# Hand-named PSUM banks and x transposed by DMA in a recurrent attention kernel

## The chip, the cores and the metric

The kernel runs on one core of a Trainium2 chip. The metric is the device time of one execution in microseconds (us); the kernel before takes 921.65 us (median of 3 runs, 919.34 to 922.05). Engines are called as in the profile: PE is TensorE (PEld its weight loads), DVE is VectorE, ACT is ScalarE, POOL is GpSimd, SP is SyncE, which here only issues DMAs.

## The reference, cut to what matters

```python
for s in range(n_seg):                          # 64 segments of 32 rows, strictly one after the other
    h = concatenate([mem, x[s*32:(s+1)*32]])    # 8 memory rows + 32 rows of x
    q, k, v = h @ Wq, h @ Wk, h @ Wv            # 32 heads of 128
    p = softmax(mask(q @ k.T * scale))
    o = (p @ v) @ Wo
    mem = o[:8]                                 # feeds the next segment
    outs.append(o[8:])
a = concatenate(outs)
b = gelu(layernorm(x) @ w1 + b1) @ w2 + b2      # independent of the recurrence
return g * a + (1 - g) * b                      # g = sigmoid(sum(x * gate_w))
```

The MLP `b` is computed first, in some 110 us. The 64 steps of the recurrence are the rest. Four steps make a *tile* of 128 rows of x.

## The kernel before

One step projects 32 rows (8 of memory, 24 of x) through Wq, Wk and Wv. The 8 rows of x left over in each of four steps are projected together for the next tile, as *side work*: units of four matmuls, 0.24 to 0.33 us each in the chain, put where PE would wait. The kernel divides PSUM, the memory that matmuls write, into eight banks. Seven rotate under one name; whoever asks takes the one used longest ago, and waits until it has been read out. The eighth holds the scores.

Some names from the code: hT is the step's transposed input, its memory rows first; QT, KT and V are its projections; E are the exponentials, R the reciprocals of their sums, Pm and Px the probabilities for memory rows and x rows; UTT is what enters the output projection and wsb what leaves it. GL are the left-over columns of a transposed tile of x, and QL, KL and VL their projections; VL takes the way through DRAM (vd).

```python
pb = loop.enter_context(tc.tile_pool(name="pb", bufs=7, space=PSUM))
ps = loop.enter_context(tc.tile_pool(name="ps", bufs=1, space=PSUM))
def bank(shape, dtype=FP32):
    return pb.tile(shape, dtype, tag="b", name="b")

def x_tr(T, x_sb):                       # x of a tile, transposed by PE
    xp = bank([P, KC, P], BF16)
    for kc in range(KC):
        nc.tensor.transpose(xp[:, kc, :], x_sb[:, kc * P:(kc + 1) * P], ident[:])
    def ev():                            # placed later in DVE's order
        ...                              # xT <- xp on DVE; GL <- left-over columns of xT on POOL
    dve_q.append(ev)
...
for s in range(nseg + 2):                # one step; the order of each engine is the order written
    ...
        prep_h(s + 1); prep_q(s); x_mul(s - 1)        # POOL: hT, QT columns, Px = E * R
    ...
            bk = bank([P, 512])                       # five Q/K banks, DVE transposes each out
    ...
            scores(S, s)                              # then two exponentials on ACT
            sm = bank([P, NG, 8])                     # sums, then run_fill(5): five side units
            run_fill(5)
            # DVE: reciprocal, Pm = E * R
            Um = [bank([P, NG, 8]) for _ in range(4)]
            av(Um, 8, s, V, Pm, 8, 0, 0)              # Pm.V for the memory rows
            sr = bank([P, NG, 32])                    # sums for the x rows
            # DVE: UTT <- Um, then the long reciprocal of sr
            run_fill(2)
    ...                                  # output projection, two halves, wsb <- wp by DVE and ACT
        if live and s >= 1:
            av_x(s - 1)                               # Px.V of the step before
        run_fill(1)
        if s + 1 < nseg:
            aT = bank([P, KC, M])                     # new memory, transposed
            ...
            nc.vector.tensor_copy(out=hn[:, :, 0:M], in_=aT[:])   # hT: the next step starts on it
            S_next = mask_mm()                        # mask into the score bank
        run_fill(1)
```

Of the kernel before, what the change touches and what calls it, by code (L numbers as in the profile page):

```python
# [23 lines left out]
def kernel(ctx, tc, A_x, A_mem0, A_Wq, A_Wk, A_Wv, A_Wo, A_seg_len, B_x, B_w1, B_b1, B_w2, B_b2, gate_w, out):  # L24
# [33 lines left out]
    x0_sb = pers.tile([P, Dm], BF16)  # L58

    with tc.tile_pool(name="mlpw", bufs=1) as mlpw, \  # L60
# [41 lines left out]
        nc.sync.dma_start(x0_sb[:], x2[0:P, :])  # L102
# [149 lines left out]
    pb = loop.enter_context(tc.tile_pool(name="pb", bufs=7, space=PSUM))  # L252
    ps = loop.enter_context(tc.tile_pool(name="ps", bufs=1, space=PSUM))
# [3 lines left out]
    def bank(shape, dtype=FP32):  # L257
        return pb.tile(shape, dtype, tag="b", name="b")
# [36 lines left out]
    dve_q, act_q = [], []  # L295

    def flush(q, n=1):
        for _ in range(min(n, len(q))):
            q.pop(0)()

    def x_load(T):
        if T == 0:
            return x0_sb
        x_sb = cw.tile([P, Dm], BF16, tag="xc", bufs=1, name="xc")
        nc.sync.dma_start(x_sb[:], x2[T * P:(T + 1) * P, :])
        return x_sb

    def x_tr(T, x_sb):
        xp = bank([P, KC, P], BF16)
        for kc in range(KC):  # L310
            nc.tensor.transpose(xp[:, kc, :], x_sb[:, kc * P:(kc + 1) * P], ident[:])

        def ev():
            xT = cw.tile([P, KC, P], BF16, tag="xT", bufs=3, name="xT")
            nc.vector.tensor_copy(out=xT[:], in_=xp[:])
            xTs[T] = xT
            GL = cw.tile([P, KC, 32], BF16, tag="GL", name="GL")
            nc.gpsimd.tensor_copy(out=GL[:].rearrange("p k (i c) -> p k i c", c=LEFT),
                                  in_=xT[:].rearrange("p k (i c) -> p k i c", c=seg)[:, :, :, RIDE:seg])
            GLs[T] = GL  # L320
        dve_q.append(ev)
# [3 lines left out]
    def left_qk(T, t, hf):  # L325
        h0, h1 = HF[hf]
        bk = bank([P, 512])
        for kc in range(KC):
            qk_unit(bk, GLs[T], t, h0, h1, kc)
            if kc < KC - 1:  # L330
                yield
        def ev():
            Tv = qk_tr(bk, h0, h1)
            if t == 0:
                nc.gpsimd.tensor_copy(out=QL[T % 2][:, h0:h1, :], in_=Tv)
            else:
                for hh in range(h0 // 8, h1 // 8):
                    r0 = 8 * hh - h0
                    nc.gpsimd.tensor_copy(out=KL[T % 2][:, :, :, hh, :], in_=Tv[:, r0:r0 + 8, :].rearrange("p g (s c) -> p g s c", c=LEFT))
        dve_q.append(ev)  # L340
        yield

    def left_v(T, vb):
        bk = bank([P, 512])
        for kc in range(KC):
            v_unit(bk, GLs[T], vb, kc)
            if kc < KC - 1:
                yield

        def ev():  # L350
            vt = cw.tile([P, 4, Dh], BF16, tag="vt", name="vt")
            nc.scalar.copy(out=vt[:].rearrange("p i e -> p (i e)"), in_=bk[:])
            if vb == 0:
                vds[T] = dr.tile([P, 4, 2, Dh], BF16, tag="vd", name="vd")
            nc.sync.dma_start(vds[T][:, 2 * vb:2 * vb + 2], vt[:].rearrange("p (a g) e -> p a g e", g=2))
            if vb == 1:
                src = vds.pop(T)[:].rearrange("(j s c) h g e -> j h c s (g e)", j=4, s=SPT)
                for j in range(4):
                    for hh in range(4):
                        r0 = 32 * j + LEFT * hh  # L360
                        nc.sync.dma_start(VL[T % 2][r0:r0 + LEFT].rearrange("p s g e -> p s (g e)"), src[j, hh])
        act_q.append(ev)
        yield

    def wo_left(T):
        bk = bank([P, Dm])
        for u in range(8):
            wo_unit(bk, UTT[T % 2], 32, u)
            if u < 7:
                yield  # L370

        def ev():
            w = cw.tile([P, Dm], BF16, tag="wsbL", bufs=1, name="wsbL")
            nc.scalar.copy(out=w[:], in_=bk[:])
            wsbLs[T] = w
        act_q.append(ev)
        yield

    def out_units(T):
        ob = bank([P, Dm])  # L380
        for si in range(SPT):
            nc.tensor.matmul(ob[32 * si:32 * si + 32, :], lhsT=SelX[:], rhs=wsbs.pop(SPT * T + si + 2)[:], start=True, stop=False,
                             tile_position=(0, 32 * si))
        yield
        if T + 3 < NT:
            x_tr(T + 3, x_load(T + 3))
            yield
        if T not in wsbLs:
            flush(act_q, 9)
        for si in range(SPT):  # L390
            nc.tensor.matmul(ob[32 * si:32 * si + 32, :], lhsT=SelL[si][:], rhs=wsbLs[T][:], start=False, stop=True,
                             tile_position=(0, 32 * si))

        def ev():
            o_sb = cw.tile([P, Dm], BF16, tag="o", bufs=1, name="o")
            nc.vector.scalar_tensor_tensor(out=o_sb[:], in0=ob[:], scalar=g_all[:, T:T + 1], in1=c_all[:, T, :], op0=ALU.mult, op1=ALU.add)
            nc.sync.dma_start(out2[T * P:(T + 1) * P, :], o_sb[:])
        dve_q.append(ev)
        yield

    def filler(T):

        if T + 1 < NT:
            for vb in range(2):
                yield from left_v(T + 1, vb)
            for hf in range(2):
                for t in range(2):
                    yield from left_qk(T + 1, t, hf)

        if T >= 1:  # L410
            yield from wo_left(T - 1)
            yield from out_units(T - 1)
        elif NT > 2:
            x_tr(2, x_load(2))
            yield
# [9 lines left out]
    def mask_mm():  # L425
        S = ps.tile([P, NG, EW], FP32, tag="S", name="S")
        nc.tensor.matmul(S[:], lhsT=ident[:], rhs=MkA[:].unsqueeze(2).to_broadcast([P, 4, 2, EW]),  # L427
                         start=True, stop=True, skip_group_check=True)
        return S

# [31 lines left out]
    m0p = bank([P, KC, M], BF16)  # L462
# [3 lines left out]
    x_tr(0, x_load(0))  # L466
    flush(dve_q)
    x_tr(1, x_load(1))
    flush(dve_q)
# [14 lines left out]
    S_next = mask_mm()  # L484
    Es, Rs, Pxs, Vs, Uxs = {}, {}, {}, {}, {}
    fill = iter(())

    def run_fill(n):
        for _ in range(n):
            if T + 1 < NT or si >= 2:  # L490
                next(fill, None)
# [10 lines left out]
    def av_x(s):  # L502
        U = [bank([P, NG, 32]) for _ in range(4)]
        av(U, 32, s, Vs.pop(s), Pxs.pop(s), 0, 32, 24)
        Uxs[s] = U

# [6 lines left out]
    for s in range(nseg + 2):  # L513
# [3 lines left out]
        if si == 0 and live:  # L517
            fill = filler(T)
        if live:
            S = S_next  # L520
            if s >= 2:
                ux_out(s - 2)
            if s + 1 < nseg and (s + 1) // SPT in xTs:
                prep_h(s + 1)
# [5 lines left out]
            for bi, (t, h0, h1) in enumerate(BANKS):  # L530
                bk = bank([P, 512])
                for kc in range(KC):
                    qk_unit(bk, hc, t, h0, h1, kc)
                Tv = qk_tr(bk, h0, h1)
                dst = QT[:, h0:h1, 0:32] if t == 0 else KT[:, h0:h1, :]
                (nc.gpsimd.tensor_copy if bi == 2 else nc.scalar.copy)(out=dst, in_=Tv)  # L536
            V = cw.tile([P, NG, Dh], BF16, tag="V", name="V")
            Vs[s] = V
            vb0, vb1 = bank([P, 512]), bank([P, 512])
# [3 lines left out]
            flush(dve_q)  # L543
# [10 lines left out]
            sm = bank([P, NG, 8])  # L554
# [8 lines left out]
            Um = [bank([P, NG, 8]) for _ in range(4)]  # L563
            av(Um, 8, s, V, Pm, 8, 0, 0)
            sr = bank([P, NG, 32])
            nc.tensor.matmul(sr[:], lhsT=BO[:], rhs=E[:, :, 16:48], start=True, stop=False, skip_group_check=True)  # L566
# [4 lines left out]
            nc.vector.reciprocal(out=R[:, 8 * NG:].rearrange("p (i q) -> p i q", q=32), in_=sr[:])  # L571
            run_fill(2)
        else:
            if s == nseg:
                ux_out(s - 2)
                x_mul(s - 1)
                av_x(s - 1)
            else:
                ux_out(s - 2)
            flush(dve_q)  # L580
            Tp, sp = divmod(s - 2, SPT)
        wsb = cw.tile([P, Dm], BF16, tag="wsb", bufs=7, name="wsb")
        for half in range(2):
            d = slice(256 * half, 256 * half + 256)
            wp = bank([P, 256])
# [5 lines left out]
        if s >= 2:  # L591
            wsbs[s] = wsb
        if live and s >= 1:
            av_x(s - 1)
        run_fill(1)
        if s + 1 < nseg:
            aT = bank([P, KC, M])
            for m in range(KC):
                nc.tensor.matmul(aT[:, m, :], lhsT=wsb[:, m * P:(m + 1) * P], rhs=Sel[:, 0:M], start=(m == 0), stop=True, skip_group_check=True)  # L599
            nc.vector.tensor_copy(out=hn[:, :, 0:M], in_=aT[:])  # L600
            S_next = mask_mm()
# [4 lines left out]
    for _ in filler(NT):  # L606
        flush(dve_q, 9)
        flush(act_q, 9)
# [12 lines left out]
    cnt = bank([1, 1])  # L621
# [121 lines left out]
```

## Time and profile before

| | kernel before |
|---|---|
| time | 921.65 us |
| span of the profiled run, mean granted PE clock | 920.6 us, 0.980 |
| PE busy | 832.7 us (90%) |
| tiles 2 to 13, mean us from each step's first score matmul to the next: steps 0-1, 1-2, 2-3, 3-0 | 12.01, 12.02, 12.18, 11.62 |
| the tile | 47.82 us |

The score matmuls come once a step, and the next scores depend on everything in between, so the distance from score to score shows where in a tile time comes or goes. The lines of the profile are in the prediction. A q behind an engine's name is its sequencer, and "issue" is time for which the profile shows no wait. In its lists "A <- B: total, times, longest" says that engine and line A waited for B. In the chain, each line is a piece of work on the path that ended last.

### The profile page before, as it was taken

To read this page: it belongs to the slowest core of one execution; us is meant where nothing else is said; L and a number is where in the kernel's file an instruction comes from. 1 tells how busy PE (TensorE), PEld (TensorE's weight loads), DVE (VectorE), ACT (ScalarE), POOL (GpSimd) and SP (SyncE) were. 2 spreads that over 40 slices of the span, in tenths; PEclk is the share of its full clock that TensorE was granted. 3 is DMA by queue.
4 is the path that set the end of the run, shared out by engine and by line. 5 is a ranking of instruction groups with operands and counts; after the bars stand their busy time and mean duration, and the time that the engine had idled before them with its cause. 6 is when DMAs were issued, how large, how long until landed. Compare 5 with 4: busy or idle time off the path is not lost.

```text
span 920.6 us, 49285 instructions
## 1 busy us (share of the span) xinstructions
PE 832.7 (90%) x22481; PEld 519.9 (56%) x22481; DVE 502.2 (55%) x999; ACT 443.2 (48%) x1252; POOL 257.1 (28%) x599
## 2 busy tenths in 40 slices
PE   1899738899999999999999999999999999999996
PEld 1566414555556566565656555656555566655554
DVE  4722214655556565556565656565656565655553
ACT  2666404454545445554544454555455545444453
POOL 1000172333333322333332323232323232323221
PEclk9999959999999999999999999999999999999998
DMA  9970001100000000010101000000000000000000
GB/s 281 421 260 1 7 1 31 27 9 26 15 27 15 27 16 26 10 32 10 32 5 37 5 27 14 28 14 23 19 21 21 15 27 15 27 15 21 10 4 17
DMA packets 29829, 37.77 MB, mean 41 GB/s; under 512 B 3592, under 2 KB 27504, under 8 KB 28080
## 3 DMA queue, kind: packets, MB, share of 16 engines
q1 hardware_dynamic: 29440, 34.30, 10.9%
q8 instruction: 178, 2.92, 1.3%
q0 software_dynamic: 176, 0.27, 0.2%
q14 instruction: 35, 0.29, 0.1%
HBM read 28.26 MB, written 6.29 MB: 38 GB/s over the span
## 4 chain that ended last, share of the span: by engine, by line
PE 81%; ACT 7%; issue 3%; DVE 3%; DMA 2%; POOL 2%; SPq 1%; ACTq 0%; POOLq 0%; DVEq 0%
PE b L269 32%; PE b L291 16%; PE b L280 12%; PE b L451 4%; PE bp L172 3%; PE hp L178 3%; ACT E L552 3%; PE b L456 2%; PE S L436 2%; PE b L566 1%; ACT wsb L590 1%; PE b L599 1%; PE b L555 1%; ACT UTT L511 1%; PE S L427 1%
## 5 line engine op out<-in xcount | busy, mean ns | idle before, releaser
L275 DVE STREAM_TRANSPOSE Tt<-b 128x512 f32<-128x512 f32 (+1 forms) x384 | 225.8, 613 | 97.4 <-PE b L269 85.1
L269 PEld LDWEIGHTS <-hT 128*32 128x32 bf16 x5120 | 134.1, 97 | 93.1 <-DVE hT L600 6.3
L291 PE MATMUL b<-Wo_sb,UTT 128*32 128x256 bf16 (+1 forms) x4736 | 166.4, 289 | 1.1 <-ACT UTT L511 0.8
L291 PEld LDWEIGHTS <-UTT 128*32 128x32 bf16 x4736 | 125.3, 98 | 26.9 <-issue 3.1
L269 PE MATMUL b<-Wq_sb,hT 128*32 128x512 bf16 x2048 | 132.9, 379 | 1.3
L280 PE MATMUL b<-Wv_sb,hT 128*32 128x512 bf16 x2048 | 133.9, 380 | 0.0
L269 PE MATMUL b<-Wk_sb,hT 128*32 128x256 bf16 (+1 forms) x3072 | 133.3, 308 | 0.0
L497 POOL TENSOR_TENSOR Px<-E,R 128x256 bf16<-128x256 bf16 x64 | 43.1, 674 | 258.1 <-DVE R L571 254.4
L571 DVE RECIPROCAL R<-b 128x256 f32<-128x256 f32 x64 | 112.0, 1749 | 4.2 <-PE b L567 4.2
L536 ACT CAST KT<-Tt 128x256 bf16<-128x256 f32 (+1 forms) x192 | 87.0, 476 | 54.1 <-DVE Tt L275 54.1
L536 POOL CAST QT<-Tt 128x512 bf16<-128x512 f32 x64 | 39.2, 612 | 189.7 <-DVE Tt L275 189.7
L590 ACT CAST wsb<-b 128x256 bf16<-128x256 f32 x66 | 24.6, 372 | 134.3 <-PE b L291 134.3
L536 ACT CAST QT<-Tt 128x512 bf16<-128x512 f32 x64 | 39.6, 618 | 98.7 <-DVE Tt L275 98.7
L511 ACT CAST UTT<-b 128x256 bf16<-128x256 f32 x256 | 77.0, 387 | 12.8 <-PE b L456 10.0
L559 DVE RECIPROCAL R<-b 128x64 f32<-128x64 f32 x64 | 35.7, 557 | 85.1 <-PE b L556 85.1
L280 PEld LDWEIGHTS <-hT 128*32 128x32 bf16 x2048 | 50.7, 96 | 28.2
L451 PEld LDWEIGHTS <-V 32*128 32x128 bf16 x4096 | 36.2, 91 | 50.8 <-DVE Pm L561 29.0
L600 DVE CAST hT<-b 128x32 bf16<-128x32 f32 x63 | 12.0, 191 | 90.3 <-PE b L599 90.3
L570 ACT CAST UTT<-b 128x64 bf16<-128x64 f32 x128 | 20.9, 215 | 77.5 <-PE b L456 77.5
L178 PE MATMUL hp<-yT,w_sb 128*128 128x256 bf16 (+1 forms) x352 | 52.5, 276 | 5.3 <-ACT hTm L179 3.5
L499 POOL TENSOR_TENSOR racc<-racc,R 128x320 f32<-128x320 f32 x64 | 55.1, 862 | 0.0
L179 ACT ACTIVATE hTm<-hp,b_sb 128x256 bf16<-128x256 f32 (+1 forms) x88 | 40.5, 470 | 29.2 <-PE hp L178 29.0
(110 smaller groups left out, 1087.1 us busy)
## 6 DMA issues: line engine op xcount, KB each, us to landing
Wq_sb<-in_A_Wq_dram SPq DMA_DIRECT2D x4, 1024.0 KB
Wk_sb<-in_A_Wk_dram SPq DMA_DIRECT2D x4, 1024.0 KB
Wv_sb<-in_A_Wv_dram SPq DMA_DIRECT2D x4, 1024.0 KB
Wo_sb<-in_A_Wo_dram SPq DMA_DIRECT2D x4, 1024.0 KB
vd<-vt SPq DMA_DIRECT2D x32, 128.0 KB
VL<-vd SPq DMA_DIRECT2D x256, 16.0 KB
out_dram<-o SPq DMA_DIRECT2D x16, 128.0 KB
xc<-in_A_x_dram SPq DMA_DIRECT2D x15, 128.0 KB
```

The source lines that it names most:

```text
L178: nc.tensor.matmul(hp[:rows, :], lhsT=w1_sb[:, kc, fc * P:fc * P + rows], rhs=yT[:, kc, :], start=(kc == 0), stop=(kc == KC - 1))
L179: nc.scalar.activation(out=hTm[:rows, fc, :], in_=hp[:rows, :], func=ACTF.Gelu_apprx_tanh, bias=b1_sb[:rows, fc:fc + 1], scale=1.0)
L269: nc.tensor.matmul(bk[32 * j:32 * j + 32, 0:n], lhsT=G[:, kc, :], rhs=W5[t][:, kc, h0:h1, j, :], start=(kc == 0), stop=(kc == KC - 1), til ...
L275: nc.vector.transpose(out=Tt[:, 0:n], in_=bk[:, 0:n])
L280: nc.tensor.matmul(bk[32 * j:32 * j + 32, :], lhsT=G[:, kc, :], rhs=Wv5[:, kc, 4 * vb:4 * vb + 4, j, :], start=(kc == 0), stop=(kc == KC - ...
L291: nc.tensor.matmul(bk[32 * g:32 * g + 32, :], lhsT=ut[:, i, j, c0:c0 + 32], rhs=Wo_sb[:, 4 * i + j, d0:d1], start=(j == 0 and i < 4), stop ...
L451: nc.tensor.matmul(U[j][:, i, :], lhsT=V[q, i, :], rhs=Pt[q, i, c_main:c_main + n], start=(i == 0), stop=False, skip_group_check=True, til ...
L497: nc.gpsimd.tensor_tensor(out=Px[:, :, 0:32], in0=E[:, :, 16:48], in1=Rr, op=ALU.mult)
L499: nc.gpsimd.tensor_tensor(out=racc[:], in0=racc[:], in1=R[:], op=ALU.add)
L511: nc.scalar.copy(out=UTT[T % 2][:, :, j, c0 + M:c0 + 40], in_=U[:])
L536: (nc.gpsimd.tensor_copy if bi == 2 else nc.scalar.copy)(out=dst, in_=Tv)
L571: nc.vector.reciprocal(out=R[:, 8 * NG:].rearrange("p (i q) -> p i q", q=32), in_=sr[:])
```

## The change

Its intent: no wait for a PSUM bank in the step. Five banks go round in the step in a written order, two serve side work, and the eighth holds in turn mask and scores, the sums, and the new memory. PE loses the transposes of x. The core of the diff:

```diff
-    pb = loop.enter_context(tc.tile_pool(name="pb", bufs=7, space=PSUM))
-    ps = loop.enter_context(tc.tile_pool(name="ps", bufs=1, space=PSUM))
+    pb = loop.enter_context(tc.tile_pool(name="pb", bufs=1, space=PSUM))
+    def bank(k, shape, dtype=FP32):
+        return pb.tile(shape, dtype, tag=f"b{k}", name=f"b{k}")
+    def side(shape, dtype=FP32):
+        side_n[0] += 1
+        while side_n[0] - 2 in side_todo:      # read-out of the bank's tenant not yet placed:
+            flush(dve_q)                       # place it here
+            flush(act_q)
+        return bank(5 + side_n[0] % 2, shape, dtype)
...
     def x_load(T):
-        if T == 0:
-            return x0_sb
-        x_sb = cw.tile([P, Dm], BF16, tag="xc", bufs=1, name="xc")
-        nc.sync.dma_start(x_sb[:], x2[T * P:(T + 1) * P, :])
-        return x_sb
+        xT = cw.tile([P, KC, P], BF16, tag="xT", bufs=3, name="xT")
+        for kc in range(KC):
+            nc.sync.dma_start_transpose(xT[:, kc, :], x2[T * P:(T + 1) * P, kc * P:(kc + 1) * P])
+        xTs[T] = xT
+        GL = cw.tile([P, KC, 32], BF16, tag="GL", name="GL")
+        nc.gpsimd.tensor_copy(out=GL[:]..., in_=xT[:]...)
...
+        if si == 1 and T + 2 < NT:
+            x_load(T + 2)                      # stands ahead of prep_h, prep_q and x_mul
...
-            sr = bank([P, NG, 32])
+            sr = B[:, 0:NG * 32].rearrange("p (i q) -> p i q", q=32)      # B: the score bank
...
+        if s + 1 < nseg:
+            S_next = mask_mm()                 # now before Px.V
         if live and s >= 1:
-            av_x(s - 1)
+            av_x(s - 1, (ne, na, nc_, nb))
         run_fill(1)
         if s + 1 < nseg:
-            aT = bank([P, KC, M])
+            aT = S_next[0][:, NG * EW:NG * EW + KC * M].rearrange("p (k m) -> p k m", m=M)
             ...
-            S_next = mask_mm()
         run_fill(1)
```

Side work is also re-dealt: the output rows of a tile are now assembled two tiles later, not one.

More of the change, by code (lines that the diff above doesn't have):

```diff
@@ L57 @@
     g_all = pers.tile([P, NT], FP32)
-    x0_sb = pers.tile([P, Dm], BF16)
     with tc.tile_pool(name="mlpw", bufs=1) as mlpw, \
@@ L101 @@
             nc.sync.dma_start(Wo_sb[:, i:i + hsplit, :], A_Wo[i:i + hsplit].rearrange("h e d -> e h d"))
-        nc.sync.dma_start(x0_sb[:], x2[0:P, :])
         make_identity(nc, ident[:])
@@ L250, with flush, later @@
                                     fill=MASK_NEG, base=M, channel_multiplier=-1)
-    pb = loop.enter_context(tc.tile_pool(name="pb", bufs=7, space=PSUM))
-    ps = loop.enter_context(tc.tile_pool(name="ps", bufs=1, space=PSUM))
+    pb = loop.enter_context(tc.tile_pool(name="pb", bufs=1, space=PSUM))
     dr = loop.enter_context(tc.tile_pool(name="dr", bufs=2, space=bass.MemoryType.DRAM))
     cw = loop.enter_context(tc.tile_pool(name="cw", bufs=2))
-    def bank(shape, dtype=FP32):
-        return pb.tile(shape, dtype, tag="b", name="b")
+    def bank(k, shape, dtype=FP32):
+        return pb.tile(shape, dtype, tag=f"b{k}", name=f"b{k}")
+    side_n, side_todo = [0], set()
+    dve_q, act_q = [], []
+    def flush(q, n=1):
+        for _ in range(min(n, len(q))):
+            k, ev = q.pop(0)
+            ev()
+            side_todo.discard(k)
+    def later(q, ev, k):
+        side_todo.add(k)
+        q.append((k, ev))
+    def side(shape, dtype=FP32):
[4 more added lines that the diff above has]
+        return bank(5 + side_n[0] % 2, shape, dtype)
     Wq5 = Wq_sb[:].rearrange("p k (h j e) -> p k h j e", h=H, j=4)
@@ L294 @@
     vds, xTs, GLs, wsbs, wsbLs = {}, {}, {}, {}, {}
-    dve_q, act_q = [], []
-    def flush(q, n=1):
-        for _ in range(min(n, len(q))):
-            q.pop(0)()
     def x_load(T):
-        if T == 0:
-            return x0_sb
-        x_sb = cw.tile([P, Dm], BF16, tag="xc", bufs=1, name="xc")
-        nc.sync.dma_start(x_sb[:], x2[T * P:(T + 1) * P, :])
-        return x_sb
-    def x_tr(T, x_sb):
-        xp = bank([P, KC, P], BF16)
-        for kc in range(KC):
-            nc.tensor.transpose(xp[:, kc, :], x_sb[:, kc * P:(kc + 1) * P], ident[:])
-        def ev():
-            xT = cw.tile([P, KC, P], BF16, tag="xT", bufs=3, name="xT")
-            nc.vector.tensor_copy(out=xT[:], in_=xp[:])
-            xTs[T] = xT
-            GL = cw.tile([P, KC, 32], BF16, tag="GL", name="GL")
-            nc.gpsimd.tensor_copy(out=GL[:].rearrange("p k (i c) -> p k i c", c=LEFT),
-                                  in_=xT[:].rearrange("p k (i c) -> p k i c", c=seg)[:, :, :, RIDE:seg])
-            GLs[T] = GL
-        dve_q.append(ev)
+        xT = cw.tile([P, KC, P], BF16, tag="xT", bufs=3, name="xT")
+        for kc in range(KC):
+            nc.sync.dma_start_transpose(xT[:, kc, :], x2[T * P:(T + 1) * P, kc * P:(kc + 1) * P])
+        xTs[T] = xT
+        GL = cw.tile([P, KC, 32], BF16, tag="GL", name="GL")
+        nc.gpsimd.tensor_copy(out=GL[:].rearrange("p k (i c) -> p k i c", c=LEFT),
+                              in_=xT[:].rearrange("p k (i c) -> p k i c", c=seg)[:, :, :, RIDE:seg])
+        GLs[T] = GL
     HF = ((0, H // 2), (H // 2, H))
@@ L326, in left_qk @@
         h0, h1 = HF[hf]
-        bk = bank([P, 512])
+        bk = side([P, 512])
+        side_k = side_n[0]
         for kc in range(KC):
@@ L339, in ev @@
                     nc.gpsimd.tensor_copy(out=KL[T % 2][:, :, :, hh, :], in_=Tv[:, r0:r0 + 8, :].rearrange("p g (s c) -> p g s c", c=LEFT))
-        dve_q.append(ev)
+        later(dve_q, ev, side_k)
         yield
     def left_v(T, vb):
-        bk = bank([P, 512])
+        bk = side([P, 512])
+        side_k = side_n[0]
         for kc in range(KC):
@@ L361, in ev @@
                         nc.sync.dma_start(VL[T % 2][r0:r0 + LEFT].rearrange("p s g e -> p s (g e)"), src[j, hh])
-        act_q.append(ev)
+        later(act_q, ev, side_k)
         yield
     def wo_left(T):
-        bk = bank([P, Dm])
+        bk = side([P, Dm])
+        side_k = side_n[0]
         for u in range(8):
@@ L375, in ev @@
             wsbLs[T] = w
-        act_q.append(ev)
+        later(act_q, ev, side_k)
         yield
     def out_units(T):
-        ob = bank([P, Dm])
+        ob = side([P, Dm])
+        side_k = side_n[0]
         for si in range(SPT):
@@ L384, in out_units @@
         yield
-        if T + 3 < NT:
-            x_tr(T + 3, x_load(T + 3))
-            yield
-        if T not in wsbLs:
-            flush(act_q, 9)
         for si in range(SPT):
@@ L397, in ev @@
             nc.sync.dma_start(out2[T * P:(T + 1) * P, :], o_sb[:])
-        dve_q.append(ev)
+        later(dve_q, ev, side_k)
         yield
@@ L403, in filler @@
         if T + 1 < NT:
-            for vb in range(2):
-                yield from left_v(T + 1, vb)
-            for hf in range(2):
-                for t in range(2):
-                    yield from left_qk(T + 1, t, hf)
+            yield from left_v(T + 1, 0)
+            yield from left_v(T + 1, 1)
+            yield from left_qk(T + 1, 0, 0)
+            yield from left_qk(T + 1, 1, 0)
+            yield from left_qk(T + 1, 0, 1)
+            yield from left_qk(T + 1, 1, 1)
+        if T >= 2:
+            yield from out_units(T - 2)
         if T >= 1:
             yield from wo_left(T - 1)
-            yield from out_units(T - 1)
-        elif NT > 2:
-            x_tr(2, x_load(2))
-            yield
     def prep_h(s):
@@ L425, in mask_mm @@
     def mask_mm():
-        S = ps.tile([P, NG, EW], FP32, tag="S", name="S")
-        nc.tensor.matmul(S[:], lhsT=ident[:], rhs=MkA[:].unsqueeze(2).to_broadcast([P, 4, 2, EW]),
+        B = bank(7, [P, 512])
+        S = B[:, 0:NG * EW].rearrange("p (i e) -> p i e", e=EW)
+        nc.tensor.matmul(S, lhsT=ident[:], rhs=MkA[:].unsqueeze(2).to_broadcast([P, 4, 2, EW]),
                          start=True, stop=True, skip_group_check=True)
-        return S
+        return B, S
     def scores(S, s):
@@ L461 @@
     nc.sync.dma_start(m0[:], A_mem0[0])
-    m0p = bank([P, KC, M], BF16)
+    m0p = side([P, KC, M], BF16)
     for kc in range(KC):
@@ L465 @@
     nc.vector.tensor_copy(out=hT[0][:, :, 0:M], in_=m0p[:])
-    x_tr(0, x_load(0))
-    flush(dve_q)
-    x_tr(1, x_load(1))
-    flush(dve_q)
+    x_load(0)
+    x_load(1)
     prep_h(0)
@@ L484 @@
     S_next = mask_mm()
+    ring = (0, 1, 2, 3, 4)
     Es, Rs, Pxs, Vs, Uxs = {}, {}, {}, {}, {}
@@ L489, in run_fill @@
         for _ in range(n):
-            if T + 1 < NT or si >= 2:
+            if T + 1 < NT or si >= 1:
                 next(fill, None)
@@ L500, in x_mul, with av_x @@
         Pxs[s] = Px
-    def av_x(s):
-        U = [bank([P, NG, 32]) for _ in range(4)]
+    def av_x(s, banks):
+        U = [bank(k, [P, NG, 32]) for k in banks]
         av(U, 32, s, Vs.pop(s), Pxs.pop(s), 0, 32, 24)
@@ L518 @@
             fill = filler(T)
+        if si == 1 and T + 2 < NT:
+            x_load(T + 2)
         if live:
-            S = S_next
+            B, S = S_next
+            na, nb, nc_, nd, ne = ring
+            ring = (nd, ne, na, nc_, nb)
+            qk_banks = (na, nb, nc_, nd, ne)
             if s >= 2:
                 ux_out(s - 2)
-            if s + 1 < nseg and (s + 1) // SPT in xTs:
+                flush(act_q)
+            if s + 1 < nseg:
                 prep_h(s + 1)
@@ L530 @@
             for bi, (t, h0, h1) in enumerate(BANKS):
-                bk = bank([P, 512])
+                bk = bank(qk_banks[bi], [P, 512])
                 for kc in range(KC):
@@ L538 @@
             Vs[s] = V
-            vb0, vb1 = bank([P, 512]), bank([P, 512])
+            vb0, vb1 = bank(na, [P, 512]), bank(nb, [P, 512])
             for kc in range(KC):
@@ L542 @@
             nc.scalar.copy(out=v_out(V, 0), in_=vb0[:])
-            flush(dve_q)
+            flush(dve_q, 9)
             for kc in range(2):
@@ L553 @@
             nc.scalar.activation(out=E[:, :, 16:EW], in_=S[:, :, 16:EW], func=ACTF.Exp, scale=scale, accum_out=hist[:, s, 1:2])
-            sm = bank([P, NG, 8])
+            sm = bank(nc_, [P, NG, 8])
             nc.tensor.matmul(sm[:], lhsT=BO[:], rhs=E[:, :, 8:16], start=True, stop=False)
@@ L562 @@
                                     in1=R[:, 0:8 * NG].rearrange("p (i q) -> p i q", q=8).unsqueeze(2).to_broadcast([P, NG, 2, 8]), op=ALU.mult)
-            Um = [bank([P, NG, 8]) for _ in range(4)]
+            Um = [bank(k, [P, NG, 8]) for k in (nd, ne, na, nc_)]
             av(Um, 8, s, V, Pm, 8, 0, 0)
-            sr = bank([P, NG, 32])
-            nc.tensor.matmul(sr[:], lhsT=BO[:], rhs=E[:, :, 16:48], start=True, stop=False, skip_group_check=True)
+            sr = B[:, 0:NG * 32].rearrange("p (i q) -> p i q", q=32)
+            nc.tensor.matmul(sr, lhsT=BO[:], rhs=E[:, :, 16:48], start=True, stop=False, skip_group_check=True)
             nc.tensor.matmul(sr[:, :, 24:32], lhsT=BO[:], rhs=E[:, :, 48:56], start=False, stop=True, skip_group_check=True)
@@ L570 @@
                 (nc.scalar.copy if j % 2 else nc.vector.tensor_copy)(out=UTT[Tp % 2][:, :, j, 24 - 8 * sp:24 - 8 * sp + M], in_=Um[j][:])
-            nc.vector.reciprocal(out=R[:, 8 * NG:].rearrange("p (i q) -> p i q", q=32), in_=sr[:])
+            nc.vector.reciprocal(out=R[:, 8 * NG:].rearrange("p (i q) -> p i q", q=32), in_=sr)
             run_fill(2)
@@ L576 @@
                 x_mul(s - 1)
-                av_x(s - 1)
+                av_x(s - 1, (ne, na, nc_, 7))
             else:
@@ L581 @@
             Tp, sp = divmod(s - 2, SPT)
-        wsb = cw.tile([P, Dm], BF16, tag="wsb", bufs=7, name="wsb")
+        wsb = cw.tile([P, Dm], BF16, tag="wsb", bufs=10, name="wsb")
         for half in range(2):
             d = slice(256 * half, 256 * half + 256)
-            wp = bank([P, 256])
+            wp = bank((nb, nd)[half], [P, 256])
             for u in range(8):
@@ L592 @@
             wsbs[s] = wsb
+        if s + 1 < nseg:
+            S_next = mask_mm()
         if live and s >= 1:
-            av_x(s - 1)
+            av_x(s - 1, (ne, na, nc_, nb))
         run_fill(1)
         if s + 1 < nseg:
-            aT = bank([P, KC, M])
+            aT = S_next[0][:, NG * EW:NG * EW + KC * M].rearrange("p (k m) -> p k m", m=M)
             for m in range(KC):
-                nc.tensor.matmul(aT[:, m, :], lhsT=wsb[:, m * P:(m + 1) * P], rhs=Sel[:, 0:M], start=(m == 0), stop=True, skip_group_check=True)
-            nc.vector.tensor_copy(out=hn[:, :, 0:M], in_=aT[:])
-            S_next = mask_mm()
+                nc.tensor.matmul(aT[:, m, :], lhsT=wsb[:, m * P:(m + 1) * P], rhs=Sel[:, 0:M], start=False, stop=True, skip_group_check=True)
+            nc.vector.tensor_copy(out=hn[:, :, 0:M], in_=aT)
         run_fill(1)
@@ L605 @@
                 pass
-    for _ in filler(NT):
+    flush(act_q, 9)
+    for _ in out_units(NT - 2):
         flush(dve_q, 9)
-        flush(act_q, 9)
+    for _ in wo_left(NT - 1):
+        pass
+    flush(act_q, 9)
+    for _ in out_units(NT - 1):
+        pass
     flush(dve_q, 9)
@@ L620 @@
     nc.vector.tensor_scalar(out=good[:, 1:2], in0=tot[:, 1:2], scalar1=RSUM_MAX, scalar2=None, op0=ALU.is_lt)
-    cnt = bank([1, 1])
+    cnt = side([1, 1])
     nc.tensor.matmul(cnt[:], lhsT=good[:, 0:1], rhs=good[:, 1:2], start=True, stop=True)
```

## The prediction

> **What bounds the kernel now.** I read the page first: busy time and the chain that ended last.
>
> ```profile
> PE 832.7 (90%) x22481; PEld 519.9 (56%) x22481; DVE 502.2 (55%) x999; ACT 443.2 (48%) x1252; POOL 257.1 (28%) x599
> ...
> PE 81%; ACT 7%; issue 3%; DVE 3%; DMA 2%; POOL 2%; SPq 1%; ACTq 0%; POOLq 0%; DVEq 0%
> ```
>
> TensorE is the bound: 81% of the chain is its own work, and no other engine is busy over 55%. So the change can gain only where TensorE stops, or where its work shrinks. The recurrence (64 steps of 32 rows, four steps to a tile of 128 rows) runs from about 155 to 905 us of 920.6. In that stretch the table by window gives PE 716.7 us busy of 750, so some 33 us of gaps.
>
> Next, the list of who waited for whom, for PE in that stretch:
>
> ```profile
> PE b L566 <- ACT UTT L570: 5.5, 15, 0.4
> PE b L451 <- ACT wsb L590: 5.3, 15, 0.4
> PE b L599 <- ACT UTT L511: 3.4, 15, 0.5
> ```
>
> Columns: total us, times, longest. Fifteen times each, so once a tile: these are waits for a PSUM bank of the seven in rotation, 14.2 us in all. That is what named banks can take away.
>
> Then the chain in order of time over one tile. The main score matmuls (L436) start at 506.36, 518.52, 530.07, 542.06 and 554.09: 12.16 us from step 2 of the tile to step 3, then 11.55, 11.99 and 12.03, together 47.7 us. I recognise step 2 because left-over Q/K work (L269) gives way there to left-over output work (L291). Its tail:
>
> ```profile
> 509.01 0.22 PE b L566
> 509.23 0.03 PE b L567
> 509.26 0.33 PE b L269 x4
> 509.59 1.99 PE b L291 x68
> 511.58 0.02 issue
> 511.60 0.38 ACT wsb L590
> 511.98 0.04 issue
> 512.02 0.35 PE b L451 x29
> 512.38 0.19 PE b L456 x8
> 512.57 0.38 ACT UTT L511
> ```
>
> Columns: start, us, what. After the output projection (L291) PE stops 0.44 us for ACT, and again 0.4 us before the new memory (L599). But starting left-over output work in a fresh bank (four of the 68) costs no wait. Last, the timeline around it:
>
> ```profile
> 508.57 0.36 PE L451 MATMUL b<-Pm,V 32*128 32x8 bf16 x32
> ...
> 509.35 1.75 DVE L571 RECIPROCAL R<-b 128x256 f32<-128x256 f32 x1
> ...
> 511.02 0.36 DVE L590 CAST wsb<-b 128x256 bf16<-128x256 f32 x1
> ...
> 512.99 0.24 PE L599 MATMUL b<-Sel,wsb 128*128 128x8 bf16 x4 [0.20 <-ACT UTT L511]
> ...
> 513.27 0.19 DVE L600 CAST hT<-b 128x32 bf16<-128x32 f32 x1 [1.89 <-PE b L599]
> ...
> 513.37 0.71 DVE L275 STREAM_TRANSPOSE Tt<-b 128x512 f32<-128x512 f32 x1
> ```
>
> DVE is held by a 1.75 us reciprocal just when PE wants banks back, and a left-over bank's transpose takes 0.71 us. These two decide my number.
>
> [...] The trace has no DMA transpose; an ordinary issue takes SP about 0.3 us.
>
> **The change part by part**, from the built instruction order.
>
> Removed: four TensorE transposes of x per tile, 0.33 us on the chain at 521.75, all on the path: -0.33 us per tile. The bank waits: in step 1 the sums wait for ACT (0.21 + 0.04, plus 0.1 in the matmuls before them) and about 0.1 us goes before the new memory: -0.5. In step 2, 0.7 us (output projection's end to new memory is 1.41 us, against 0.72 in step 0): -0.7. Every tenant of the ring of five is read out long before reuse: the five Q/K banks by DVE while the next ones fill, both V banks by ACT before the output projection, the Px·V banks by ACT one after another, each ahead of the Q/K bank that takes it.
>
> Moved: the mask matmul (0.21 us) goes from behind the new memory to before Px·V. Behind, it filled the time DVE needs to copy the new memory: copy at 0.28 us after the matmuls' start, 0.19 long, next Q/K at about 0.6. Now only one unit of side work (0.24 us) or none fills it: +0.1 us in steps 0, 1 and 2, +0.2 in step 3, so +0.5 per tile. One side unit that was x's transpose frees its slot, already counted.
>
> So far -0.33 - 0.5 - 0.7 + 0.5 = about -1.0 us per tile: -16 us in all.
>
> Added: side work gets two banks only, in turn, and a bank is reused only after its tenant's read-out is *placed* in an engine's order. Where it isn't yet, it is placed on the spot. Walking PE's and DVE's orders through a tile:
> - Steps 0, 1 and 3: the earlier tenant is read out in time. In step 1 the third Q/K group waits for a transpose placed behind the first wsb copy: the copy ends near 511.4, the transpose near 512.1, PE arrives about 512.1: +0.1.
> - Step 2, the two units behind the sums: the second starts the output rows of tile T-2 in side bank 6, whose tenant finished in the five units before. Its transpose is placed in DVE's order *behind the 1.75 us reciprocal*. In the timeline's frame PE arrives at 508.57 + 0.37 + 0.24 + 0.22 = 509.4; DVE ends the reciprocal at 511.1 and the transpose at 511.75; PE resumes near 511.8. PE is in order, so the 64 matmuls of the output projection stand behind: +2.4 us.
> - Step 2, the unit after the new memory: left-over output work takes bank 5, whose transpose stands behind the hT copy. Matmuls' start + 0.28 + 0.19 - 0.08 + 0.71 = 1.1, then 0.24 of work: Q/K starts at 1.4 us instead of 0.65: +0.75.
>
> Together +3.25 us for tiles 2 to 14 (13 of them); tile 1 has the first only; tile 0 neither. The units of output work are also re-dealt: step 2 gets two of the longer ones and step 3 loses its last two; no net change.
>
> Per tile -1.0 + 3.25 = +2.2; 13 x 2.2 = +29; tile 1 +1; tiles 0 and 15 -1 each; a longer tail (another output block after the loop, two groups of 0.33 us) +0.7: **+28 us**.
>
> x by DMA: SP issues the four transposes behind the first vd copy (534.2 in the tile shown), about 534.6; [...]landing 1.6 after the last issue, as for VL[...]. GpSimd's copy of the left-over columns now stands at the head of its work in step 1 (from 537.0), ahead of QL, Px and Q work for the scores. That chain is 0.29 + 0.27 + 0.40 + 1.84 + 0.61 = 3.4 us long and the scores need it 5.05 us after the start, so up to 1.65 us (538.6) is free. It just fits; I add 0.1 us x 14, say 1.5 us, and put the danger into the range. In the preamble the eight transposes lie beside GpSimd's mask building, which ends at 130.7: free.
>
> Sum: 921.65 + 28 + 1.5 = **951 us**.
>
> **The rivals.**
> 1. *The waits simply go.* If the placed transposes do no harm, about -1.0 to -1.3 us per tile: 901 to 905 us. For it: the bank waits are real, and a hand-named order was surely made to remove them. Against it: the built order has the transpose behind the reciprocal, and PE's first matmul in the bank carries a wait for DVE.
> 2. *The DMA transpose comes late.* Each us beyond 538.6 stops the scores for as long, 14 times. Landing at 541 would add 33 us: about 985. For it: four issues to one queue and an estimate without a trace. Against it: [...]idle DMA engines (7% busy in the loop).
> 3. *The side-bank wait is shorter*, partly recovered because GpSimd and ACT catch up while PE stands: +1.5 instead of +3.25 per tile, 928 us: same. Against: step 2's path after it is PE's own.
>
> **Range and chances.** 951 us, 930 to 975. The low end is rival 3 with all gains; the high end has DMA transposes 1.7 us late in each tile. Faster by over 2% (under 903) needs rival 1 whole: 0.06. Within 2%: 0.22. Slower by over 2% (above 940): 0.72.
>
> **What would show it.** Right: once a tile (13 or 14 times) the output-row or left-over output matmul waits some 2.4 us for a DVE transpose, and once 0.7 to 1 us behind the hT copy; score starts 11.2 to 11.6 us apart in steps 1 and 3, near 15 in step 2; no waits of the sums or Px·V for ACT. Wrong: GpSimd's GL copy waiting for DMA with the scores waiting for GpSimd (rival 2); or score distances of 11 to 12 us throughout (rival 1).

The forecast came to 921.65 + 28 + 1.5 = 951 us. Passages in it are cut, as marked, that no trace or run of this case shows: what was said of DMA transposes and of matmuls that share a bank, and the speed held against rival 2.

## The result

The changed kernel takes **1026.53 us** (median of 4 runs, 1025.41 to 1028.76), against 921.11 us for the kernel before in 4 runs. The ratio is 1.115, 95% interval 1.1124 to 1.1176. Ratios here are the mean time of one kernel's fast runs over that of the other's of the same rounds, so not quite the ratio of the medians quoted.

The prediction said slower, 951 us, with 975 as the high end. The direction was right and the size was not: +105 us where +29 were forecast.

The page of the changed kernel, busy time and chain:

```profile
PE 866.9 (85%) x22417; PEld 523.2 (51%) x22417; DVE 496.6 (48%) x983; ACT 445.8 (44%) x1252; POOL 254.4 (25%) x599
...
PE 67%; SPq 8%; DVE 6%; POOL 5%; DMA 5%; ACT 5%; issue 3%; POOLq 0%; ACTq 0%; DVEq 0%
```

PE's share of the chain fell from 81% to 67%. New on the chain are SP's queue with 8% and DMA with 5%. And PE shows 34 us *more* busy time with 64 matmuls fewer, although no matmul grew. Both will need an explanation.

Whom PE waited for in the recurrence of the changed kernel (total us, times, longest):

```profile
PE b L387 <- DVE Tt L293: 28.1, 13, 2.2
PE b L437 <- POOL QT L542: 27.9, 14, 2.0
PE b L309 <- DVE Tt L293: 13.9, 14, 2.2
PE b L437 <- POOL QT L422: 10.7, 13, 2.0
```

The three bank waits for ACT of the kernel before are gone, as intended. In their place are waits of side work (L387 output rows, L309 left-over output) for DVE's transpose, and of the scores (L437) for POOL. Once a tile each.

The step distances say where in the tile it happens (means of tiles 2 to 13, us):

| steps | before | predicted for the change | measured |
|---|---|---|---|
| 0-1 | 12.01 | 12.1 | 13.29 |
| 1-2 | 12.02 | 11.2 to 11.6 | 15.20 |
| 2-3 | 12.18 | near 15 | 15.44 |
| 3-0 | 11.62 | 11.2 to 11.6 | 11.30 |
| tile | 47.82 | 50.0 | 55.22 |

Two of the predicted figures are worked out from its terms: 12.1 is 12.0 plus its 0.1 for the mask, and 50.0 is 47.7 plus 2.2 and 0.1. Steps 2 and 3 came near. The miss is in step 1, where the DMA transposes are: its scores come late in two parts, so that it shows in the distances 0-1 and 1-2 both (the first score matmul waits for QT by 0.8 us in the mean, 10.7 / 13, and the second half of them by another 2.0, 27.9 / 14).

**Step 2, the forecast stop.** The chain in order of time, changed kernel, one tile (start, us, what):

```profile
508.25 0.21 ACT UTT L576
...
508.50 1.76 DVE R L577
510.25 0.58 DVE Tt L293
...
510.88 0.40 PE b L387 x4
511.28 3.33 PE b L309 x64
...
515.88 0.19 DVE hT L608
516.07 0.63 DVE Tt L293
...
516.74 0.40 PE b L309 x4
```

This is the walk of the prediction, in its order: the long reciprocal, the side bank's transpose behind it, then PE. The 64 matmuls behind the waiting four start only after them, at 511.10 by the timeline, though the last UTT copies before them had ended by 508.57. Later the hT copy, again a transpose, then PE. But one line is not in it: the output projection (L309, 64 matmuls) takes 3.33 us, where it took 1.99 for 68 before. Nothing is waited for inside it. The table by window gives the granted clock (columns: window, us, busy us of PE, PEld, DVE, ACT, POOL with counts, clock, DMA share, GB/s):

```profile
508.40:511.00 2.60, 0.44 (x8) 0.14 (x12) 2.42 (x4) 0.17 (x2) 0.11 (x1) 1.00 0.00 0
511.00:514.60 3.60, 3.60 (x69) 2.47 (x61) 0.42 (x1) 0.00 (x0) 0.50 (x1) 0.53 0.02 5
...
567.20:569.00 1.80, 1.80 (x68) 1.54 (x57) 0.42 (x1) 0.00 (x0) 0.24 (x1) 1.00 0.00 0
```

After a stop of about 2.2 us PE's clock was half for some 3.4 us: a granted clock of 0.53 over 511.0 to 514.6, and 0.50 over 511.24 to 514.65. One tile later the same stop cost no clock, and the projection took 1.75 us. In this trace the first stretches at half rate in the recurrence start at 159.67, 214.28 and 231.35 us, 16 and 5 times 3.41 us apart, which is the length of the slow stretch above. The 3.41 us before that stretch, 507.83 to 511.24, hold the whole stop, with PE busy for 1.25 us. One tile later, counted on from 511.24 in lengths of 3.41 us, the stop is divided between two of them, 562.44 to 565.86 and 565.86 to 569.27, with PE busy for 2.21 and 2.46 us, and the clock stayed at 1.00. So much do these two tiles show; that this is why it came once and once not was not shown. The prediction had left the clock out.

**Step 1, the miss.** The same chain from the end of step 0 into step 1, two tiles later:

```profile
591.83 0.34 SPq L358
...
592.27 1.69 SPq L317
...
594.01 1.22 SPq L317
...
595.28 1.22 SPq L317
...
596.54 3.22 DMA xT<-in_A_x_dram
...
599.91 0.06 POOL GL L320
...
600.36 0.40 POOL QT L422
...
602.47 0.56 POOL QT L542
...
603.08 0.28 PE b L437 x16
```

SP issues the first vd copy (L358) and then the DMA transposes (L317), over 1.2 us each. The last one's issue and landing take 3.22 us. POOL stands at GL (L320) until then, and only afterwards does the work that the scores need: QT, Px, and the last QT of the score's operand. The list of POOL's waits gives 182.7 us in 14 times for GL behind the DMA. Most of that is idle time of an idle engine; what costs is what the scores then wait: 27.9 + 10.7 = 38.6 us. In the tile shown the granted clock from 603 to 607 us, after this stop, was 0.57.

### The profile page after: what moved, and what is told of

Read it like the earlier page. It is cut to its first block, busy times and chain, and to the rows that moved or that the text cites. A ratio compares the mean times of both kernels' runs of the same rounds, so it can differ in the third digit from the quotient of the medians.

```text
span 1024.7 us, 49290 instructions
## 1 busy us (share of the span) xinstructions
PE 866.9 (85%) x22417; PEld 523.2 (51%) x22417; DVE 496.6 (48%) x983; ACT 445.8 (44%) x1252; POOL 254.4 (25%) x599
## 4 chain that ended last, share of the span: by engine, by line
PE 67%; SPq 8%; DVE 6%; POOL 5%; DMA 5%; ACT 5%; issue 3%; POOLq 0%; ACTq 0%; DVEq 0%
PE b L287 24%; PE b L309 13%; PE b L298 9%; SPq L317 6%; DMA xT<-in_A_x_dram 4%; PE b L452 3%; PE bp L170 3%; PE hp L176 3%; DVE R L577 2%; PE b L457 2%; ACT E L558 2%; DVE Tt L293 2%; PE b L437 2%; PE b L428 1%; PE b L561 1%
## 5 line engine op out<-in xcount | busy, mean ns | idle before, releaser
L309 PE MATMUL b<-Wo_sb,UTT 128*32 128x256 bf16 (+1 forms) x4736 | 172.7, 298 | 15.3 <-DVE Tt L293 13.9
L309 PEld LDWEIGHTS <-UTT 128*32 128x32 bf16 x4736 | 129.7, 101 | 46.4 <-issue 14.1
L298 PE MATMUL b<-Wv_sb,hT 128*32 128x512 bf16 x2048 | 138.1, 388 | 0.0
L337 POOL CAST QL<-Tt 128x512 bf16<-128x512 f32 x32 | 19.7, 616 | 191.0 <-DVE Tt L293 191.0
L287 PE MATMUL b<-Wq_sb,GL 128*32 128x512 bf16 x512 | 52.3, 479 | 17.0 <-POOL GL L320 17.0
L298 PEld LDWEIGHTS <-hT 128*32 128x32 bf16 x2048 | 51.9, 97 | 27.5
L437 PE MATMUL b<-QT,KT 128*32 128x40 bf16 x2048 | 28.5, 182 | 38.6 <-POOL QT L542 27.9
```

Of the source, the lines that this page charges most:

```text
L287: nc.tensor.matmul(bk[32 * j:32 * j + 32, 0:n], lhsT=G[:, kc, :], rhs=W5[t][:, kc, h0:h1, j, :], start=(kc == 0), stop=(kc == KC - 1), til ...
L298: nc.tensor.matmul(bk[32 * j:32 * j + 32, :], lhsT=G[:, kc, :], rhs=Wv5[:, kc, 4 * vb:4 * vb + 4, j, :], start=(kc == 0), stop=(kc == KC - ...
L309: nc.tensor.matmul(bk[32 * g:32 * g + 32, :], lhsT=ut[:, i, j, c0:c0 + 32], rhs=Wo_sb[:, 4 * i + j, d0:d1], start=(j == 0 and i < 4), stop ...
L437: nc.tensor.matmul(S[32 * j:32 * j + 32, i, M:M + 40], lhsT=KT[:, h, :], rhs=QT[:, h, :], start=False, stop=True, skip_group_check=True, t ...
```

## The experiments

Ten kernels ran, all reported correct. The kernel before was run beside each group (medians 920.2 to 920.7 us).

### The GL copy moved out of the way

```diff
-        GL = cw.tile(...); nc.gpsimd.tensor_copy(...)      # in x_load, at the start of step 1
+        if si == 2 and T + 2 < NT:
+            gl_copy(T + 2)                                 # the same copy, before the output projection of step 2
```

> Change kept whole, only GpSimd's copy of the left-over columns (GL) of the DMA-transposed tile moves from the start of step 1 to step 2, so no GpSimd work for the scores stands behind the DMA. My theory (the late DMA transpose stops GpSimd, GpSimd stops the scores, and the stop halves the TensorE clock for some us): the two steps around it fall by about 4.65 us a tile, 14 tiles, so 1026.5 - 65 = about 961 us, step distances 12.1, 11.6, 14.8 to 16.3, 11.3. Rival (the DMA transposes hurt by themselves: SP's queue, or the traffic): stays over 1000.

Measured: 967.93 us (966.41 to 971.83), ratio to before 1.0524. Steps 12.44, 11.72, 15.68, 11.30. So 58.6 us of the 105 belong to POOL standing behind the DMA. In the list of PE's waits both lines for POOL are gone. The transposes as such are still there, as slow as ever (median issue 1.23 us), and cost nothing that this run shows. The rival falls.

### Plain loads instead of DMA transposes

```diff
-            nc.sync.dma_start_transpose(xT[:, kc, :], x2[...])
+            nc.sync.dma_start(xT[:, kc, :], x2[...])
```

> Wrong result on purpose: the four DMA transposes of a tile become four plain loads of the same blocks, in the same place, GL copy left at the start of step 1. My theory (each transpose takes SP 1.2 to 1.7 us to issue and 2 to 3 us to land, where a plain load takes 0.3 and 1.6): lands within the 1.65 us that GpSimd has free, so about 961 us as with GL moved. Rival (any DMA issued behind the first vd copy comes too late): over 1000.

Measured: 971.91 us (967.60 to 976.98), ratio 1.0572. The run was meant to be wrong and was still reported correct: the comparison with the reference does not see a tile of x whose blocks are untransposed, so here "correct" says nothing about the path of x. For timing it serves. SP's issues of the two kernels, transposes first (duration in ns, least, median, greatest):

```profile
L317 SPq DMA_TRANSPOSE xT<-in_A_x_dram x64: 1101/1231/2252, 111.2 to 870.6; - x64
```

```profile
L317 SPq DMA_DIRECT2D xT<-in_A_x_dram x64: 350/430/1444, 111.3 to 815.0; - x64
```

A transpose costs SP 1.23 us to issue, a plain load of the same block 0.43. Four issues make 4.9 us against 1.7. In the recurrence the four take longer than that sum, since one or two of them do: 5.9 us against 2.4 from the first start to the last end (medians of 14 tiles). With plain loads the DMA just about fits, as I had worked out for the transposes: six tiles still waited at the last QT, 5.7 us in all. So a landing about 3 us earlier is nearly enough; the position behind the vd copy by itself costs some 4 to 6 us, by the 4 between the medians of this run and the last, whose ranges overlap, and by the 5.7 of waits.

### The transposes issued earlier

```diff
+        if si == 0 and T + 2 < NT:
+            x_load(T + 2)                # before the first vd copy in SP's order
         if si == 1 and T + 2 < NT:
-            x_load(T + 2)
+            gl_copy(T + 2)               # GL stays at the head of step 1
```

> The change, with the four DMA transposes issued at the start of step 0 instead of behind the first vd copy; GpSimd's GL copy stays at the head of step 1. My theory (only the lateness of the landing at that place costs): as with GL moved, about 966 us. Rival (the transposes, or GL ahead of the score work, cost by themselves): 985 us or more.

Measured: 966.53 us (966.08 to 966.86), ratio 1.0499. The same gain, with GL where the change had put it. Three ways to have the data there before POOL asks, or nearly so, give 966 to 972 us. Lateness is the whole cost; neither the place of GL nor the transposes' traffic has a part that these runs can see.

### The side banks read out earlier

```diff
+            flush(dve_q)                                    # behind Pm
             Um = [bank(k, [P, NG, 8]) for k in (nd, ne, na, nc_)]
...
             (nc.scalar.copy if half else nc.vector.tensor_copy)(out=wsb[:, d], in_=wp[:])
+            if half == 0:
+                flush(dve_q)                                # behind the first wsb copy
```

> Change kept whole with its late DMA; only DVE's read-out of the finished side bank is placed earlier, behind Pm and behind the first wsb copy, so no side matmul waits for a transpose behind the 1.75 us reciprocal or the hT copy. My theory: step 2 falls from a mean of 15.6 to about 11.6 us, 13 tiles: 1026.5 - 52 = about 975 us. Rival (the stop in step 2 only hid other lateness, or the extra transpose ahead of the UTT copies costs as much): over 1000.

Measured: 976.40 us (971.39 to 978.22), ratio 1.0584. Steps 13.75, 15.19, 11.68, 11.35: step 2 fell from 15.44 to 11.68, nothing else moved by more than 0.5. The waits of side work for DVE's transpose are out of the list of the longest. The rival, a stop that only hid other lateness, falls.

### Both edits

> Both edits together: GL copy late and read-outs early. If the two costs are all there is and independent, about 46.6 us a tile against 47.7 before: 903 to 910 us, faster than the kernel before by 1 to 2%. Rival (named banks gain nothing by themselves, the mask's move eats it): 921 us or more.

Measured: 911.60 us (909.64 to 915.10), ratio 0.9902, interval 0.9871 to 0.9933. Steps 12.46, 11.67, 11.66, 11.30, the tile 47.09 us. The two costs together make 1026.5 - 911.6 = 115 us. The edits alone took 58.6 and 50.1 us, in sum 109: nearly independent. The named banks and x by DMA together do gain, 0.7 us a tile; the prediction had put that at 1.0 us. Against the kernel before, steps 1-2, 2-3 and 3-0 are 0.36, 0.52 and 0.32 us shorter, but 0-1 is 0.45 longer. The prediction had +0.1 there, and what the rest is was not traced.

### The mask matmul alone

```diff
+        if s + 1 < nseg:
+            S_next = mask_mm()
         if live and s >= 1:
             av_x(s - 1)
...
-            S_next = mask_mm()            # from behind the hT copy, in the kernel before
```

> The kernel before, with one edit: the mask matmul moves from behind the new memory's matmuls to before the Px.V matmuls, as the change has it. It measures the term I booked at +0.5 us a tile. My theory (behind, it hid part of DVE's hT copy): 921 + 16 x 0.5 = about 929 us. Rival (it costs nothing, since PE had to wait for ACT's wsb copy there anyway in steps 1 and 2): 921, or a little under.

Measured: 931.27 us (928.17 to 932.81), ratio 1.0131, interval 1.0112 to 1.0149. A tile is 48.44 us against 47.82, +0.6 where +0.5 was booked. A 0.21 us matmul that looked movable had been covering DVE's copy: from the new memory's first matmul to the next Q/K matmul it is 0.60 us before (512.99 to 513.59), with the mask in between, and still 0.54 with the mask gone (588.28 to 588.82). By steps it is +0.22, +0.23, -0.07 and +0.25, so in step 2 it cost nothing, as the rival had it. The change writes the mask into the shared bank first and the new memory behind it, and the move came with that, so this is a price of sharing as it was done here. Whether another order would serve was not tried.

### x by DMA alone

The kernel before, with its seven rotating banks; only the x path of the change, with GL late.

> The kernel before with its seven banks in rotation; only x is transposed by DMA, with the GL copy late (step 2). If taking four 0.33 us transposes per tile off TensorE is all that the DMA brings: 921 - 15 x 0.33 = 916 us, and a bank less in the rotation may bring some tenths more per tile. Rival (the slow DMA transposes disturb VL's and vd's loads): 921 or more.

Measured: 923.07 us (921.28 to 925.33), ratio 1.0036, interval 1.0019 to 1.0054: not faster. My expectation missed. The list of PE's waits shows a new first entry (L376 is the second half of the output rows):

```profile
PE b L376 <- ACT wsbL L362: 6.7, 15, 1.2
```

PE's transposes used to stand between the two halves of the output rows and gave ACT the time for its wsbL copy. The 15 x 0.33 us taken away are spent waiting for ACT instead. That accounts for the missing gain. Why the kernel is even 2.9 us slower I have not traced; steps 0-1 are 0.24 us longer. Whether the DMA transposes have a part in that stays open.

### x by PE in the mended kernel

The mended change, with x transposed by PE in a side bank again, as the last side unit of a tile.

> The mended change with x transposed by TensorE again, in a side bank. Splits the mended kernel's gain into banks and DMA: 911.6 + 14 x 0.33 = about 916 us if the DMA brings just TensorE's time; 921 or more if the DMA brings all the gain and the named banks none.

Measured: 913.99 us (913.12 to 914.38), ratio 0.9936. It is 2.4 us slower than with the DMA, where 4.6 were expected, and still faster than the kernel before. Against the kernel before that is 0.6% of gain with PE's transposes and 1.0% with the DMA. By these figures about two thirds of the mended gain come without the DMA, from the banks and the re-dealt side work, and one third with it. That is rough: the intervals of the two ratios overlap (0.9921 to 0.9951 here), and a tile is 47.18 us against 47.09.

### Side work behind the new memory

```diff
             av_x(s - 1, (ne, na, nc_, nb))
-        run_fill(1)
         ...
             nc.vector.tensor_copy(out=hn[:, :, 0:M], in_=aT)
-        run_fill(1)
+        run_fill(2)
```

> The mended change (GL late, read-outs early), with the unit of side work from before the new memory's matmuls moved behind them, so that two units cover the hT copy there. If the uncovered copy costs 0.1 us in three steps of a tile: 911.6 - 16 x 3 x 0.1 = about 907 us. Rival (the new memory then waits for ACT's second wsb copy instead): 911 to 915 us.

Measured: 900.25 us (897.50 to 901.86), ratio 0.9783, interval 0.9764 to 0.9803. Steps 12.20, 11.41, 11.38, 11.32: about 0.26 us in each of the first three steps, more than twice the 0.1 expected. The uncovered hT copy had been a larger loss than I had read from the chain.

### Side work in front of the sums

```diff
+            run_fill(1)                    # PE waits here for the first exponential
             sm = bank(nc_, [P, NG, 8])
...
             nc.vector.reciprocal(out=R[:, 8 * NG:]..., in_=sr)
-            run_fill(2)
+            run_fill(1)
```

> The fastest version so far (GL late, read-outs early, side unit behind the new memory), with one of the two side units behind the sums moved in front of the first sum, where TensorE waits some 0.5 us for the first exponential. If that wait is bare and the unit behind the sums covered nothing: 0.24 us a step in some 60 steps, 900 - 14 = about 886 us. Rival (behind the sums it covered the long reciprocal, so the mask and Px.V matmuls now wait instead): 897 to 903 us.

Measured: **889.41 us** (887.43 to 889.93), ratio 0.9663, interval 0.9649 to 0.9676. Steps 12.01, 11.21, 11.21, 11.17. It is the fastest version, 3.4% faster than the kernel before. In its chain no ACT piece stands between scores and sums any more. The mended kernel first (scores, exponential, sum), then this one:

```profile
512.25 0.13 PE b L443 x8
...
512.46 0.38 ACT E L562 x2
...
512.88 0.19 PE b L565
```

```profile
510.53 0.23 PE b L439 x32
510.76 0.08 PE b L443 x8
510.84 0.65 PE b L298 x12
511.49 0.14 PE b L566
```

The scores (L439, L443) are followed by 12 matmuls of L298, eight for V and the four of a side unit, and then directly by the first sum (L566), where the mended kernel, like the kernel before, had the 0.38 us exponential between.

## Why the prediction was right or wrong, point by point

- **Slower rather than faster: right**, and for a reason it named. The bank waits went, and a larger wait came from where a read-out was placed in DVE's order.
- **The side-bank stop of 2.4 us in step 2 and of 0.75 behind the hT copy: right in place and size.** In tiles of the GL-late kernel whose clock stayed full, steps 2-3 took 14.78 us, against 11.66 with the read-outs early: 3.1 us, where 3.15 were booked for the two. The count (13 and 14 times) was right too.
- **The DMA transposes' term (1.5 us): the step that failed.** The prediction put the first issue at 534.6 and the landing 1.6 us after the last, as for VL (1.64 us at 147.58 in the trace of the kernel before), and said "It just fits". By these figures the four issues had 2.4 us until 538.6, or 0.6 each; that they would keep within it was my estimate. The mechanism, POOL standing at GL and the scores behind POOL, was the rival's and is what happened. The size was off: an issue is 1.23 us, so four take 4.9 us or more, where 2.4 were left. And in the tile shown the last one's issue and landing make 3.22 us together. From the first issue to GL it was 7.4 us (median of 14 tiles), where 4.0 were free (534.6 to 538.6). The direct cost is 38.6 us of score waits instead of 1.5. The rival had its arithmetic nearly right: "Each us beyond 538.6 stops the scores for as long". 3.4 us late cost 2.8 us of waits a tile. It was given too little weight, because an estimate stood in for a duration that no trace had.
- **A term missing from every version of the sum: PE's clock.** The mean granted clock is 0.980 before, 0.946 in the changed kernel, 0.970 with GL late and 0.982 with both edits. If all lost clock is half rate, the time at half rate is 2 x (1 - clock) x span: 37 us before, 111 in the changed kernel, 58 with GL late, 33 with both edits. The clock records in these traces hold no values but 1 and 0.5, and at 0.5 they add up to 39, 113, 60 and 35 us, so the rule holds here. Some 33 to 37 us of half-rate time are thus in the kernel before and in the mended one, most of it before the recurrence (in the kernel before 111.99 to 135.88 us, clock 0.50); the changed one has 74 us on top of the kernel before. If PE has work throughout, that loses half: by my estimate from these 74 us, up to 37. It would also account for PE's 34 us of extra busy time.
- **The sum, as measured.** From the changed kernel to GL late: 58.6 us, of which 38.6 are the scores' waits; the other 20 fit the clock (111 - 58 = 53 us at half rate, up to 27 lost). From GL late to both edits: 56.3 us, of which the stops are 13 x 3.1 = 40 and tile 1's 2.4; the other 14 fit the clock (25 us, up to 12 lost) only roughly. The clock's share is inferred from the granted clock and from tiles of one run with and without it (with GL late, steps 2-3 took 14.78 us with the clock at 1 throughout, and 16.1 to 16.7 with 3.4 us at half rate). No run changed the clock alone.
- **The moved mask (+0.5): right in sum**, +0.6 alone, but not step by step (+0.22, +0.23, -0.07, +0.25 where +0.1, +0.1, +0.1, +0.2 were booked). **The gain of the banks and the transposes (-1.0 net): somewhat too high**, -0.7. One reading behind it was off: before the new memory PE stood for 0.20 us, as the prediction's own timeline says, not 0.4; four side matmuls (L291, 512.38) ran in between.
- **Rival 3 (the stop is partly recovered): wrong.** With a full clock the stops cost their length (3.1 us), and with a halved one more, not less (with GL late, steps 2-3 took 16.1 to 16.7 us against 14.78).

## What to carry to other kernels

Before a producer is replaced by a slower one, work out when its result lands against the first consumer in *program order*; here POOL stood at GL for the DMA 14 times, did the scores' work behind it only afterwards, and the scores waited 38.6 us. A hand-made buffer scheme needs the read-outs placed by hand too: the read-out behind the 1.75 us reciprocal here made PE wait 28.1 us in 13 times. And a PE stop of about 2.2 us cost more than its length here in some tiles: after it the granted clock was 0.50 from 511.24 to 514.65 us in one, and 1.00 in the next. Once its waits were placed the change gave 1%; the banks and the re-dealt side work gave 0.6% without the DMA, and the DMA nothing by itself in the kernel before. Placing two side units where PE still waited gave a further 2.4 points; whether the kernel before would gain as much from that was not tested.
